# Earlier and wider-spaced stack loads, and a later exponential, in a two-block attention kernel

## The chip, the core and the metric

The kernel runs on one core of a Trainium2 chip. The metric is the device time of one execution in microseconds (us). Engines are named as the profile names them: PE (matmuls; PEld is its weight loads), DVE (VectorE), ACT (ScalarE), POOL (GpSimd) and SP (SyncE, which issues nearly all DMAs here).

## The reference, cut to what matters

Two attention blocks on separate inputs, each 2048 positions of width 640, 32 heads of 20 values. Block A looks at 8 earlier positions, two apart; block B is full attention.

```python
def _A_ref(x, wqkv, wo):                       # H=32, Dh=20, W=8, dil=2
    q, k, v = ...                              # x @ wqkv, split in heads
    idx = pos[:, None] - arange(W)[None, :] * dil
    logits = einsum("bhsd,bhswd->bhsw", q, k[idx]) * scale
    attn = softmax(where(idx >= 0, logits, -1e9))
    return einsum("bhsw,bhswd->bhsd", attn, v[idx]) @ wo

def _B_ref(x, wqkv, wo):
    q, k, v = ...
    p = softmax(einsum("bhqd,bhkd->bhqk", q, k) * Dh ** -0.5)
    return einsum("bhqk,bhkd->bhqd", p, v) @ wo

return concatenate([_A_ref(...), _B_ref(...)], axis=-1)
```

All inputs are float32.

## The kernel before

**Stages.** The projections of both blocks come first (to about 440 us of the profiled execution). They leave q, k and v of both blocks in DRAM scratch tensors (`qa_d`, `ka_d`, `va_d`, `qb_d`, `kb_d`, `vb_d`). Then one loop over 512 steps (`for i in range(NS + LAG)`) does all of block B's attention, and block A's attention is woven into it. Block B's output projection follows (from about 1800 us).

**Block B's loop.** The 32 heads form 8 groups of 4. A group has 4 query chunks of 512 and each chunk 16 key blocks of 128, so a group is 64 steps and a chunk 16. `g` is the group of step `i` and `sub` its step within the group. A step does:

- `b_qk(i)`: four score matmuls (`ps_st<-bq,bk`) and four exponentials on ACT (`e<-ps_st`).
- `b_pv(i - 2)`: the products with the values (`ps_st<-e,vb`). Every second step ACT copies the sum out (`more<-ps_st`) and POOL adds it to the running one (`braw<-braw,more`).
- `b_max(i + 24)`: matmuls of a later chunk (`ps_mx<-bk,bq`), of which DVE takes the row maxima (`mx<-ps_mx`). They are needed before that chunk's exponentials.

The matmuls read **stacks**: `bk` (the keys of a group), `bq` (its queries, by chunk) and `vb` (its values), two buffers of each. Of group g+1 the maxima read `bk` and the first chunk of `bq` from `sub` 40 of group g on. The score matmuls read them from `sub` 0 of group g+1.

**Two side chains of each chunk.** Both go through DRAM and so through SP's queue:

- *Maxima* (`max_rows`): DVE reduces and transposes them (`mtr<-mx`), POOL splits them, SP stores them (`mdr<-mtr`, 4 DMAs) and loads them back as two extra rows of `bq` (`bq<-mdr`, 2 DMAs). That load is due 3 steps before the chunk's first score matmul, which reads it.
- *Normalizing* (`normalize`): SP stores the sums (`s_d<-braw`, due at steps 6, 22, 38 and 54 of a group) and loads them in another layout (`sm<-s_d`, a step later). DVE takes the reciprocal two steps after that (`sm<-sm`). SP stores and broadcasts it (`s_d<-sm`, `rb<-s_d`) and POOL multiplies.

**Order of the work.** Each engine runs its instructions in the order in which the program issues them. `after(n, fn)` puts a call off by n steps; `tick()` at the head of a step runs the calls that are due, in the order in which they were put off. So SP's queue is the order of these calls, and a DMA that has to wait holds up all behind it.

**Block A in the loop.** `a_attention` is a generator of 128 units, 4 for the scores and 4 for the values of each of 16 tiles of 128 positions, nearly all of it POOL work (`akv`, `ao`). `next(a_work)` runs one unit at the steps with `i % 14` in 1, 5, 7, 11. Each unit also moves `a_softmax` of the open tile on by one `yield`: the maximum (DVE `am<-al`), the subtraction (POOL `al<-al,am`), the exponential (ACT `al<-al`), the sums (POOL `am<-al`, `am<-am`), the reciprocal (DVE `am<-am`), the product (POOL). What is left of it when the tile's first unit of values comes (`c == 4`) is run at once there. For tiles 1 to 14 eight units lie between the last scores and that unit, for the first and the last tile only four. Block A's output projection (`a_out`, 15 matmuls `ps_st<-ww,aot` and an ACT copy `ro<-ps_st`) is put into single steps with `i % 6 == 4`.

**The lines that change.** `a_softmax` has one `yield` between the subtraction and the exponential. The loop calls `b_pieces(g + 1)` at `sub == 16` and puts off 21 loads: 4 pieces of `bk` (640, 352, 640, 352 KB), 16 pieces of `bq` (160 and 80 KB in turn) and one of `vb` (760 KB), one each step, so at `sub` 16 to 36.

Of the kernel before, what the change touches and what calls it, by code (L numbers as in the profile page):

```python
# [22 lines left out]
NG = H // GH  # L23
# [35 lines left out]
def attention_pair(ctx, tc, xa, wqk_a, wv_a, wo_a, xb, wqk_b, wv_b, wo_b, oa, ob):  # L59
# [12 lines left out]
    def after(n, fn, *args):  # L72
        due.setdefault(now[0] + n, []).append((fn, args))
# [7 lines left out]
    def tick():  # L81
        now[0] += 1
        for fn, args in due.pop(now[0], ()):
            fn(*args)
# [232 lines left out]
    def pool(out, a, b, op):  # L317
        gp.tensor_tensor(out, a, b, op)
# [12 lines left out]
    def a_softmax(t):  # L331

        _, L, _ = a_t[t]
        if t % (NT // 2) == 0:
            pool(L, L, mask, ALU.add)
        yield
        yield
        m = sb.tile([128, 4, H], F32, tag="am", bufs=2, name="am")
        dve.tensor_reduce(m[:, 0], L.rearrange("p o h -> p h o"), AX.X, ALU.max)
        yield  # L340
        pool(L, L, m[:, 0].unsqueeze(1).to_broadcast([128, WIN, H]), ALU.subtract)
        yield
        act.activation(L, L, AF.Exp, scale=SCALE)
        yield
        pool(m, L[:, :4], L[:, 4:], ALU.add)
        pool(m[:, :2], m[:, :2], m[:, 2:], ALU.add)
        pool(m[:, 0], m[:, 0], m[:, 1], ALU.add)
        yield
        dve.reciprocal(m[:, 0], m[:, 0])
        yield  # L350
        pool(L, L, m[:, 0].unsqueeze(1).to_broadcast([128, WIN, H]), ALU.mult)
# [46 lines left out]
    def a_turn(t, o):  # L398

        b = sb.tile([128, KC, 128], F32, tag="stg", bufs=3, name="turn")  # L400
        d = dr.tile([128, D], F32, tag="tr_d", bufs=2, name="tr_d")

        def back():
            r = sb.tile([128, KC, 128], F32, tag="stg", bufs=3, name="back")
            src = d.rearrange("(b j) (k m c) -> m j k b c", b=4, k=KC, c=32)
            for m in range(4):
                sp.dma_start(r[32 * m:32 * m + 32].rearrange("j k (b c) -> j k b c", c=32), src[m])
            turned.append((now[0] + 3, t, r))
        for k in range(KC):
            after(1 + k, dve.transpose, b[:, k], o[:, k * 128:(k + 1) * 128])  # L410
        after(KC + 2, sp.dma_start, d, b.rearrange("p k c -> p (k c)"))
        after(KC + 5, back)

    def turn_parts():

        if ready_a or not turned or turned[0][0] > now[0]:
            return
        _, t, r = turned.pop(0)
        ot = sb.tile([128, 2, KC, 128], F32R, tag="aot", bufs=1, name="aot")
        gp.tensor_copy(ot[:, 0], r)  # L420
        gp.tensor_tensor(ot[:, 1], r, ot[:, 0].bitcast(F32), ALU.subtract)
        ready_a.append((now[0] + 7, t, ot))
# [62 lines left out]
    def b_pieces(g):  # L485
        k = sb.tile([128, 2, S], F32R, tag="big", bufs=4, name="bk")
        q = sb.tile([128, NQC, 2, 512], F32R, tag="big", bufs=4, name="bq")
        v = sb.tile([128, NKB, VG], F32, tag="vb", bufs=2, name="vb")
        stacks[g] = (q, k, v)
        out = []  # L490
        hs = [slice(g * GH + 2 * r, g * GH + 2 * r + 2) for r in range(2)]

        def add(t, src, runs):
            for r0, s0, n in runs:
                out.append(lambda: sp.dma_start(t[r0:r0 + n].bitcast(F32), src[s0:s0 + n]))
        for r in range(2):
            for r0, s0, n in BK_RUNS:
                add(k[r * HALF:], kb_d[:, hs[r]], [(r0, s0, n)])
        for qc in range(NQC):
            for r in range(2):  # L500
                for r0, s0, n in BQ_RUNS:
                    add(q[r * HALF:, qc], qb_d[qc, :, hs[r]], [(r0, s0, n)])
        return out[:4], out[4:]

    def v_piece(g, b0, b1):

        sp.dma_start(stacks[g][2][:, b0:b1], vb_d[b0 * 128:b1 * 128, g * GH * VC:g * GH * VC + VG]
                     .rearrange("(b p) c -> p b c", p=128))
# [134 lines left out]
    def b_qk(i):  # L643
        u, kb = divmod(i, NKB)
        g, qc = divmod(u, NQC)
        q, k, v = stacks[g]
        P[i] = []
        for pl in range(2):
            w = wide() if pl and i + LEAD >= NS else None
            ps2 = [bank() for _ in range(2)] if w is None else [w[:, 0], w[:, 1]]  # L650
            for r in range(2):
                rows = slice(r * HALF, r * HALF + BM)
                pe.matmul(ps2[r], k[rows, pl, kb * 128:kb * 128 + 128], q[rows, qc, pl], start=True, stop=True)
            if i + LEAD >= NS and i % 2:
                e = sb.tile([128, 2, 512], F32, tag="akv", bufs=4, name="e")
            else:
                e = sb.tile([128, 2, 512], F32, tag="p", bufs=PB, name="e")
            for r in range(2):
                act.activation(e[:, r], ps2[r], AF.Exp, scale=SCALE)
                if w is None:  # L660
                    give(ps2[r])
            P[i].append(e)
            yield

    def b_pv(i):
        u, kb = divmod(i, NKB)
        g, qc = divmod(u, NQC)
        n, part = divmod(kb, 2)
        if part == 0:
            accs[u] = bank()  # L670
        acc = accs[u]
        for j in range(GH):
            pe.matmul(acc[32 * j:32 * j + 32, :], stacks[g][2][:, kb, j * VC:j * VC + 32], P[i][j % 2][:, j // 2],
                      start=(part == 0), stop=(part == 1))
        del P[i]
        if part == 0:
            return
        if n == 0:
            raws[u] = sb.tile([128, 512], F32, tag="raw", bufs=2, name="braw")
            act.copy(raws[u], acc)  # L680
        else:
            more = spare[n % 2][:, n // 2 % 2]
            act.copy(more, acc)
            after(1, pool, raws[u], raws[u], more, ALU.add)
        give(accs.pop(u))
        if kb == NKB - 1:
            last = g == NG - 1
            normalize(raws.pop(u), g, qc * 512, 2 if last else 5, (lambda: out_last(qc)) if last else None)
# [4 lines left out]
    def out_first(qc):  # L693

        o = columns(2)
        outs_b[qc] = o
        for k in range(KC - 1):
            after(1 + 2 * k, split, chunk(o, 0, k), chunk(o, 1, k),
                  ot_b[k * 128:(k + 1) * 128, qc * 512:(qc + 1) * 512], "stg", gp, gp.tensor_copy)
# [71 lines left out]
    def load_out(src, W, halves=range(2)):  # L771
        for h in halves:
            w, more = wide_pieces(src[h], gp)
            W.append(w)
            loads.extend(more)
# [16 lines left out]
    loop[0] = now[0] + 1  # L792
    for i in range(NS + LAG):
        g, sub = divmod(i, NQC * NKB)
        if sub == 16 and g + 1 < NG:
            k_loads, q_loads = b_pieces(g + 1)
            for n, fn in enumerate(k_loads + q_loads + [lambda g=g + 1: v_piece(g, 0, NKB)]):
                after(1 + n, fn)
        if i in (NS - 56, NS - 40):
            out_first((i - NS + 56) // NKB)  # L800
        tick()
        if loads and i % 2:
            loads.pop(0)()
        if i % 14 in (1, 5, 7, 11) and next(a_work, 0) == 0:
            for d in done_a:
                d[0] -= 1
        if done_a and done_a[0][0] <= 0:
            a_turn(*done_a.pop(0)[1:])
        turn_parts()
        if i + LEAD >= NS:  # L810

            for _ in b_qk(i) if i < NS else ():
                pass
            if i % 2:
                b_pv(i - LAG - 1)
                b_pv(i - LAG)
                if fill:
                    fill.pop(0)()
            continue
        qk = b_qk(i) if i < NS else iter(())  # L820
        next(qk, None)
        if i >= LAG:
            b_pv(i - LAG)
        else:
            v_group(*v_late.pop(0))
            if not v_late:
                load_out(wo_a, WO, (1,))

                spare += [sb.tile([128, 2, 512], F32, tag="last0", bufs=2, name="more") for _ in range(2)]
        next(qk, None)  # L830
        mx = b_max(i + LEAD)
        next(mx, None)
        if fill and i % 2 == 0:
            fill.pop(0)()
        elif i % 6 == 4 and not out_piece() and not left_a[0] and not WO_b:
            load_out(wo_b, WO_b)
        next(mx, None)
# [57 lines left out]
```

## Time and profile before

| | us |
|---|---|
| median of 3 runs | 1849.35 |
| the 3 runs | 1849.69, 1845.63, 1849.35 |
| the profiled execution, its own time | 1847.92 |
| its span, first to last instruction | 1846.1 |
| busy: PE / DVE / ACT / POOL | 1797.0 / 1319.3 / 1352.8 / 1214.2 |
| mean granted clock of PE | 0.998 |

The profile's page gives each engine's busy time and share of the span. The view of windows gives the same for stretches of 20 us. The view of waits adds up who waited for whom. The timeline lists instructions in order of time: start, duration, engine, operation, tile written and read, how many alike were merged (x4), and in brackets the idle time of the engine before it and what ended it. "SPq" rows are SP issuing DMAs; their duration is that of issuing, not of moving the data.

### The profile page before, as it was taken

The page shows a single profiled execution, that of the slowest core. Times are in us where ns is not written, and L with a number is a line of the kernel's source. Part 1 is how long each engine was busy: PE and PEld are TensorE (multiplying, and loading weights), DVE is VectorE, ACT ScalarE, POOL GpSimd, SP SyncE. Part 2 cuts the span into 40 slices and gives each one's busy share as a digit, 9 for nine tenths or more (in the row PEclk, how much of TensorE's full clock was granted, in tenths as well). Part 3 has the DMA queues.
Part 4 walks back from the last instruction along what each step waited for, and adds up shares of the span by engine and source line. Part 5 has one row for each costly group of instructions (what it writes and reads, how often), then busy time and mean ns, then how long its engine had stood idle before and what let it go on. Part 6 is the DMA issues. An engine that isn't in the chain of part 4 may idle for free. (4 is left out here: it accounts for less than half of the span.)

```text
span 1846.1 us, 30585 instructions
## 1 busy us (share of the span) xinstructions
PE 1797.0 (97%) x11211; PEld 961.3 (52%) x11211; DVE 1319.3 (71%) x1350; ACT 1352.8 (73%) x2597; POOL 1214.2 (66%) x1072
## 2 busy tenths in 40 slices
PE   9999999999999999999999999999999999999999
PEld 8888888886334343343343333433434434433568
DVE  3100233278898989988989999899888898899500
ACT  4222322224898989988989999899888898899891
POOL 0000075028999999989899899899988873255232
PEclk9999999999999999999999999999999999999999
DMA  6323686655552364336425633553363242021023
GB/s 223 111 93 110 204 301 235 217 170 179 143 154 96 99 180 136 101 114 171 123 83 153 172 96 104 158 153 108 101 189 111 72 119 75 18 69 52 27 70 112
DMA packets 193006, 240.23 MB, mean 130 GB/s; under 512 B 90972, under 2 KB 121308, under 8 KB 191864
## 3 DMA queue, kind: packets, MB, share of 16 engines
q1 hardware_dynamic: 192280, 237.63, 42.7%
q8 instruction: 88, 1.44, 0.3%
q10 hardware_dynamic: 576, 0.66, 0.1%
q14 instruction: 62, 0.51, 0.1%
HBM read 173.29 MB, written 64.91 MB: 129 GB/s over the span
## 5 line engine op out<-in xcount | busy, mean ns | idle before, releaser
L55 DVE TENSOR_REDUCE mx<-ps_mx 128x2 f32<-128x1024 f32 x1024 | 1196.8, 1217 | 139.0 <-PE ps_mx L55 136.7
L55 ACT ACTIVATE e<-ps_st 128x512 f32<-128x512 f32 x2000 | 1061.0, 606 | 57.0 <-PE ps_st L55 27.9
L55 PE MATMUL ps_st<-e,vb 128*32 128x512 f32 x4096 | 544.1, 605 | 0.5
L55 PE MATMUL ps_st<-bq,bk 62*128 62x512 f32 x2000 | 470.8, 455 | 2.6 <-ACT e L55 2.6
L55 PEld LDWEIGHTS ps_st<-bq,bk 62*128 62x128 f32 x2000 | 246.9, 184 | 425.2 <-ACT e L55 411.7
L55 PE MATMUL ps_mx<-bk,bq 60*128 60x512 f32 x2048 | 422.3, 442 | 39.9 <-DVE mx L55 23.4
L55 POOL TENSOR_TENSOR braw<-braw,more 128x512 f32<-128x512 f32 x224 | 287.5, 1284 | 182.7 <-ACT more L55 176.9
L55 POOL TENSOR_TENSOR akv<-akv,aq 128x1280 f32<-128x1280 f32 x64 | 188.1, 2939 | 237.1 <-DMA akv<-ka_d 237.1
L55 PEld LDWEIGHTS ps_mx<-bk,bq 60*128 60x128 f32 x2048 | 193.0, 185 | 208.5 <-DVE mx L55 197.7
L55 POOL TENSOR_TENSOR akv<-akv 128x640 f32<-128x640 f32 (+3 forms) x304 | 281.7, 927 | 23.8
L55 PEld LDWEIGHTS ps_st<-e,vb 128*32 128x32 f32 x4096 | 82.1, 108 | 157.8 <-ACT e L55 81.9
L55 ACT COPY ro<-ps_st 128x320 f32<-128x320 f32 (+1 forms) x92 | 43.5, 473 | 156.8 <-PE ps_st L55 111.6
L55 POOL TENSOR_TENSOR akv<-akv,al 128x1280 f32<-128x1280 f32 x64 | 151.5, 2366 | 0.2
L55 ACT COPY more<-ps_st 128x512 f32<-128x512 f32 x224 | 132.4, 591 | 12.6 <-PE ps_st L55 5.8
L55 PE MATMUL ps_st<-ww,xn 128*128 128x320 f32 x720 | 120.1, 315 | 0.0
L55 PEld LDWEIGHTS ps_st<-ww,xn 128*128 128x128 f32 x720 | 106.6, 188 | 20.9 <-ACT e L55 9.1
L55 POOL TENSOR_TENSOR xn<-stg,xn 128x512 fp32r<-128x512 f32 (+1 forms) x20 | 30.1, 1507 | 96.1 <-ACT xn L55 94.9
L55 DVE TENSOR_TENSOR wc<-stg,wc 128x480 fp32r<-128x480 f32 (+5 forms) x15 | 8.4, 559 | 102.2 <-ACT wc L55 102.1
L55 PE MATMUL ps_st<-ww,aot 128*128 128x320 f32 x480 | 79.7, 318 | 0.0
L55 PEld LDWEIGHTS ps_st<-ww,aot 128*128 128x128 f32 x480 | 71.2, 190 | 12.0 <-ACT e L55 5.5
L55 POOL TENSOR_TENSOR ao<-ao,akv 128x640 f32<-128x640 f32 x48 | 74.7, 1557 | 3.8
L55 DVE TENSOR_TENSOR xl<-stg,xl 128x512 fp32r<-128x512 f32 x12 | 8.3, 688 | 95.9 <-ACT xl L55 95.9
(84 smaller groups left out, 1313.9 us busy)
## 6 DMA issues: line engine op xcount, KB each, us to landing
akv<-ka_d SPq DMA_DIRECT2D x128, 320.0 KB
akv<-va_d SPq DMA_DIRECT2D x128, 320.0 KB
kb_d<-pr SPq DMA_DIRECT2D x20, 512.0 KB
qb_d<-pr SPq DMA_DIRECT2D x20, 512.0 KB
bk<-kb_d SPq DMA_DIRECT2D x16, 640.0 KB
bq<-qb_d SPq DMA_DIRECT2D x64, 160.0 KB
rb<-s_d SPq DMA_DIRECT2D x128, 64.0 KB
stg<-xb SPq DMA_DIRECT2D x12, 512.0 KB
```

Source lines behind the costliest of these rows:

```text
L55: return lambda *a, **k: self.tc.keep_in_program_order(op(*a, **k))
```

## The change

The loads of the next group's stacks are put off from `sub == 4` on, and one is due every second step: the pieces of `bk` at `sub` 4, 6, 8, 10, those of `bq` at 12 to 42, `vb` at 44. In `a_softmax` there is one `yield` more between the subtraction and the exponential, so the exponential and all that follows it come one unit of block A later.

```diff
@@ -339,6 +339,7 @@
         dve.tensor_reduce(m[:, 0], L.rearrange("p o h -> p h o"), AX.X, ALU.max)
         yield
         pool(L, L, m[:, 0].unsqueeze(1).to_broadcast([128, WIN, H]), ALU.subtract)
+        yield
         yield
         act.activation(L, L, AF.Exp, scale=SCALE)
         yield
@@ -792,10 +793,10 @@
     loop[0] = now[0] + 1
     for i in range(NS + LAG):
         g, sub = divmod(i, NQC * NKB)
-        if sub == 16 and g + 1 < NG:
+        if sub == 4 and g + 1 < NG:
             k_loads, q_loads = b_pieces(g + 1)
             for n, fn in enumerate(k_loads + q_loads + [lambda g=g + 1: v_piece(g, 0, NKB)]):
-                after(1 + n, fn)
+                after(1 + 2 * n, fn)
         if i in (NS - 56, NS - 40):
             out_first((i - NS + 56) // NKB)
         tick()
```

## The prediction

> **What bounds the kernel now.** I read the page first, then the waits of the loop (440 to 1740 us), then the windows for stretches that fall behind, then the timeline there. The page puts PE at 97%, but that busy time is modelled, so I looked at what paces an ordinary stretch of the loop:
>
> ```profile
> PE 1797.0 (97%) x11211; PEld 961.3 (52%) x11211; DVE 1319.3 (71%) x1350; ACT 1352.8 (73%) x2597; POOL 1214.2 (66%) x1072
> ...
> 905.32 0.59 ACT L55 COPY more<-ps_st 128x512 f32<-128x512 f32 x1 [0.19 <-PE ps_st L55]
> ...
> 905.80 4.38 ACT L55 ACTIVATE e<-ps_st 128x512 f32<-128x512 f32 x8
> ...
> 910.25 0.59 ACT L55 COPY more<-ps_st 128x512 f32<-128x512 f32 x1
> ```
>
> From one `more` copy to the next, which is two steps, pass 910.25 - 905.32 = 4.93 us, and ACT is busy in them for 0.59 + 4.38 = 4.97 us. So in ordinary steps ACT sets the pace, and time in which ACT stands still there is time lost. That is my unit of price. Neither half of the change shortens ACT's work; it can only remove or add stalls. The waits of the loop have two entries that the change touches:
>
> ```profile
> ACT al L55 <- POOL al L55: 2.4, 1, 2.4
> ...
> DVE sm L55 <- DMA sm<-s_d: 3.1, 2, 1.9
> ```
>
> One wait of block A's exponential for POOL, and two waits of DVE for the sums that come back from DRAM. Each holds an engine that runs in order, and so the whole loop.
>
> **The exponential.** In the first group POOL was late with the subtraction, and ACT stood before the exponential:
>
> ```profile
> 497.66 0.72 POOL L55 TENSOR_TENSOR al<-al,am 128x256 f32<-128x256 f32 x1
> ...
> 498.40 0.42 ACT L55 ACTIVATE al<-al 128x256 f32<-128x256 f32 x1 [2.42 <-POOL al L55]
> ...
> 499.36 0.49 PE L55 MATMUL ps_st<-bq,bk 62*128 62x512 f32 x1 [1.88 <-ACT e L55]
> ...
> 502.95 1.08 ACT L55 ACTIVATE e<-ps_st 128x512 f32<-128x512 f32 x2 [0.71 <-PE ps_st L55]
> ...
> 506.49 0.43 ACT L55 COPY ro<-ps_st 128x320 f32<-128x320 f32 x1 [2.45 <-PE ps_st L55]
> ...
> 587.41 0.43 ACT L55 COPY ro<-ps_st 128x320 f32<-128x320 f32 x1 [1.56 <-PE ps_st L55]
> ...
> 500.00:520.00 20.00, 19.46 (x124) 8.52 (x121) 15.95 (x19) 16.10 (x33) 19.06 (x17) 0.91 0.56 163
> ```
>
> ACT lost 2.42 us, then 0.71, and then at the output projection 2.45 us where the same place later costs 1.56 (row 587.41), so 0.89 more: 2.42 + 0.71 + 0.89 = 4.0 us. The last column but two of the windows row says why there is an aftermath: the granted clock was 0.91 there, PE ran slow after its own wait of 1.88 us. The Trainium skill ("TensorE: Matmul & The Clock Gate", Part 1 and "HAM oscillation") says that PE falls to half clock for a window of about 3.4 us, and only after gaps longer than about 3.4 us. The size agrees, 1 - 0.5 x 3.4 / 20 = 0.915, the threshold does not: 1.88 us was enough. By the page's threshold the aftermath would be chance and this term 2.4 instead of 4.0 us; I go by the rows.
>
> With the added yield the subtraction stays at `i % 14 == 5` and the exponential moves from 7 to 11, so POOL has six steps (some 15 us at 4.93 per two) instead of two. A delay of 2.42 us is covered: **-4.0 us**. The sums, the reciprocal and the product move by a unit too; from sums to reciprocal it stays 4 steps, so DVE has no new wait behind POOL. The exception is tile 15, with four units between: now the exponential, the sums and the reciprocal all fall into one unit, and DVE must wait in its queue, with all later maxima behind it, for ACT and POOL:
>
> ```profile
> 1470.32 0.47 POOL L55 TENSOR_TENSOR am<-al 128x128 f32<-128x128 f32 x1
> ...
> 1470.87 0.65 POOL L55 TENSOR_TENSOR am<-am 128x64 f32<-128x64 f32 x2
> ```
>
> 0.42 + 0.47 + 0.65 = 1.5 us at most, nothing if DVE comes later than ACT by as much. I take the middle, **+0.8 us**. The same at tile 0, before the loop, lies under projection matmuls that do not wait for DVE's next instruction; at nothing, and 1.5 us if that cover fails.
>
> **The loads.** Both DVE waits lie where the 21 pieces are issued now:
>
> ```profile
> 843.25 0.55 SPq L55 DMA_DIRECT2D s_d<-braw  x1
> ...
> 849.56 0.35 SPq L55 DMA_DIRECT2D sm<-s_d  x1
> ...
> 851.20 0.25 DVE L55 RECIPROCAL sm<-sm 128x16 f32<-128x16 f32 x1 [1.17 <-DMA sm<-s_d]
> ...
> 854.85 1.09 ACT L55 ACTIVATE e<-ps_st 128x512 f32<-128x512 f32 x2 [1.42 <-PE ps_st L55]
> ...
> 1347.67 0.54 SPq L55 DMA_DIRECT2D s_d<-braw  x1
> ...
> 1355.74 0.35 SPq L55 DMA_DIRECT2D sm<-s_d  x1
> ...
> 1358.55 0.25 DVE L55 RECIPROCAL sm<-sm 128x16 f32<-128x16 f32 x1 [1.90 <-DMA sm<-s_d]
> ...
> 1362.54 1.08 ACT L55 ACTIVATE e<-ps_st 128x512 f32<-128x512 f32 x2 [2.49 <-PE ps_st L55]
> ...
> 1364.44 0.59 ACT L55 COPY more<-ps_st 128x512 f32<-128x512 f32 x1 [0.82 <-PE ps_st L55]
> ```
>
> From the store of the sums to their load passed 6.3 and 8.1 us, and DVE was held 1.17 and 1.90 us. ACT then lost 1.4 us at the first place and 2.49 + 0.82 = 3.3 us at the second. What makes SP slow there is the pieces:
>
> ```profile
> 651.31 0.36 SPq L55 DMA_DIRECT2D bk<-kb_d  x1
> 651.71 1.46 SPq L55 DMA_DIRECT2D ot_b<-braw  x4
> 653.21 1.99 SPq L55 DMA_DIRECT2D bk<-kb_d  x1
> 655.25 1.00 SPq L55 DMA_DIRECT2D akv<-ka_d  x2
> 661.39 0.67 SPq L55 DMA_DIRECT2D bk<-kb_d  x2
> ...
> SPq L55 <- DMA bk<-kb_d: 5.1, 1, 5.1
> ```
>
> SP issued eight DMAs from 651.31 on (1 + 4 + 1 + 2) and then stood 5.1 us, by the waits, for a `bk` piece. I read it so: the ninth DMA waits until the first has landed, which took 661.39 - 651.31 = 10.1 us. With a piece in every step, SP runs into that again and again and the sums come late. The Trainium skill ("DMA: Bandwidth & Descriptors", Specifications) gives about 27 GiB/s for a DMA engine, and its rule on how many engines a DMA uses gives ten for 40 rows: 640 KB would be some 2.3 us, by estimate. By that figure the pieces could not hold SP and the waits would stay (first rival); the 10.1 us speak against it.
>
> At half the rate a piece of `bk` has 4.93 us to itself, and at `sub` 22 and 38 only `bq` pieces of 160 and 80 KB are left beside the sums. So both waits go: **-1.4 - 3.3 = -4.7 us**. What is late next? Three places, of which I cost two at nothing and one not.
>
> At `sub` 6 to 9 the big pieces now meet the sums of the chunk before; they come singly and the reciprocal waits for program order three steps (7.4 us) behind the store: nothing, 3.3 us a time if not. At `sub` 44 `vb` is queued directly before the stores of the maxima, which lead to `bq<-mdr` and so to the first score matmul at 48. The nearest rows are `vb` before a store of sums, and that load with its reader:
>
> ```profile
> 1555.32 0.39 SPq L55 DMA_DIRECT2D vb<-vb_d  x1
> 1555.80 1.32 SPq L55 DMA_DIRECT2D s_d<-braw  x1
> 1560.89 0.32 SPq L55 DMA_DIRECT2D sm<-s_d  x1
> ...
> 1241.20 0.53 SPq L55 DMA_DIRECT2D bq<-mdr  x2
> ...
> 1246.73 0.40 PE L55 MATMUL ps_st<-bq,bk 62*128 62x512 f32 x2
> ```
>
> Store to load behind `vb` took 5.1 us in all. The load at 1241.20 had 5.5 us to its reader; a load from DRAM took 851.20 - 849.56 = 1.6 us to be usable, which leaves 3.9. Were all 5.1 us added, it would be 1.2 us late here, the tightest of the seven places that I looked at; but part of the 5.1 us the maxima take without `vb` too. Nothing, with 1.2 us as the bad end.
>
> In the first group there is no room. Its load at `sub` 15 comes just in time:
>
> ```profile
> 481.23 0.53 SPq L55 DMA_DIRECT2D bq<-mdr  x2
> ...
> 482.99 0.64 PE L55 MATMUL ps_st<-bq,bk 62*128 62x512 f32 x2 [0.74 <-ACT e L55]
> ```
>
> 1.8 us before its reader. Two pieces now stand in SP's queue shortly ahead of it, at 0.36 us of issuing each (row 651.31) and a little of their data: **+0.8 us**, between nothing and the 3.3 us of the worst stall above.
>
> The sum is -4.0 - 4.7 + 0.8 + 0.8 = **-7.1 us**. Against the profiled execution's own 1847.92 us that is 1840.8. That execution lies 1.4 us under the median of the runs, so against the median it is 1849.35 - 7.1 = **1842.3 us**.
>
> **The rivals.** *The reciprocal's waits only move* to `sub` 9 or 41, or the pieces were never their cause. For it: the three normalizations that the pieces now touch in each group instead of one. Against: half the rate. Then -4.0 + 1.6 = -2.4 us, 1846.9.
>
> *The maxima come late* (the other side). The `bk` pieces at 8 and 10 and `vb` at 44 stand before `mdr` and `bq<-mdr`, and PE, ACT and DVE wait at `sub` 16 and 48. Mechanism: SP held for the eighth DMA before, as at 656.25. It decides from about 3.9 us of added delay, and one hold was 5.1 us. If it costs 1 us at one place in each of six groups, with the 1.6 us of slow clock that followed the first stall (0.71 + 0.89), it is 6 x 2.6 = 15.6 us, so 1849.35 - 7.1 + 15.6 = 1857.9. Against: SP reaches these stores only every 16 steps, and the load then has over 5 us.
>
> *The stalls are chance.* The three runs span 4 us with one program; the fastest, 1845.63, may hold none of the three stalls. Then the median moves by about half, to some 1846.
>
> **How the numbers follow.** About 0.2%, 3.7 us, is what a measurement of this kernel can tell from no change. Chances: the forecast 0.55 (faster), the waits that move 0.20 (same), the late maxima 0.15 (slower), chance stalls 0.10 (half faster, half same). So faster 0.60, same 0.25, slower 0.15. The low end is the fastest run less the sum, 1845.6 - 7.1 = 1838.5. The high end takes in the forecast with its bad ends (-8.7 + 1.5 + 3.3, 1845.5) and the rival of 1846.9, and reaches 1851 into the late maxima, leaving out most of these.
>
> **What would show it.** Right: in the waits of the loop no `ACT al <- POOL al` and no `DVE sm <- DMA sm<-s_d`, SP's waits for `bk<-kb_d` well under their present length, no window below 1.00 in the clock, `bq<-mdr` still several us before its reader. Wrong: an idle PE or ACT at the first score matmul of a chunk (steps 16 and 48), a reciprocal held at `sub` 9 or 41, or DVE held for POOL's sums other than once, at the last tile.

## Result and profile after

The changed kernel takes 1841.84 us (median of 7 runs, 1841.37 to 1843.49) against 1847.59 us before (7 runs, the three above among them, 1844.03 to 1849.69). The ratio is 0.9972 [0.996, 0.9984], so it is faster: the gain of 0.28% is small, but its interval leaves out 1. The profiled execution went from 1847.92 to 1841.84 us and its span from 1846.1 to 1840.0, 6.1 us less.

The engines' busy times on the page of after are nearly those of before:

```profile
PE 1796.4 (98%) x11211; PEld 961.8 (52%) x11211; DVE 1318.5 (72%) x1350; ACT 1356.7 (74%) x2597; POOL 1214.9 (66%) x1072
```

As no engine has less work, the 6.1 us are stalls. The waits of the loop after (total, number of times, longest) no longer hold the two rows of before, `ACT al <- POOL al` and `DVE sm <- DMA sm<-s_d`. Of PE, DVE and ACT two others of 0.4 us or more are new:

```profile
PE ps_st L55 <- DMA bq<-mdr: 2.0, 1, 2.0
...
DVE am L55 <- POOL am L55: 0.4, 1, 0.4
```

SP's own waits for pieces of `bk` in the loop, first before and then after:

```profile
SPq L55 <- DMA bk<-kb_d: 55.9, 19, 5.1
```

```profile
SPq L55 <- DMA bk<-kb_d: 0.5, 1, 0.5
```

SP stood 55.9 us for them in 19 waits, and now 0.5 in one.

**The exponential.** The timeline of after, at the place of the 2.42 us wait:

```profile
498.16 0.72 POOL L55 TENSOR_TENSOR al<-al,am 128x256 f32<-128x256 f32 x1
...
504.65 0.43 ACT L55 COPY ro<-ps_st 128x320 f32<-128x320 f32 x1 [1.55 <-PE ps_st L55]
...
510.04 0.42 ACT L55 ACTIVATE al<-al 128x256 f32<-128x256 f32 x1
```

POOL's subtraction ends at 498.88 and the exponential starts at 510.04 without a wait. The copy `ro` waits the ordinary 1.55 us instead of 2.45.

**The sums.** The timeline of SP and DVE after, at the place of the second wait (group 5):

```profile
1339.78 0.53 SPq L55 DMA_DIRECT2D s_d<-braw  x1
1340.41 2.69 SPq L55 DMA_DIRECT2D back<-tr_d  x4
1343.20 0.58 SPq L55 DMA_DIRECT2D sm<-s_d  x1
...
1353.52 0.24 DVE L55 RECIPROCAL sm<-sm 128x16 f32<-128x16 f32 x1
```

From the end of issuing the store to the load pass 2.9 us, where it was 7.5. The store itself also goes out sooner: 4.3 us ahead of the first score matmul of its step, where it came 0.5 us behind it. The reciprocal does not wait. At this place (`sub` 22) the seven groups that load a next one had 4.3 to 7.9 us before and have 1.2 to 2.9 after. I call this time the store-to-load gap below.

**The new stall.** In the first group, step 16, after:

```profile
477.39 0.67 SPq L55 DMA_DIRECT2D bq<-qb_d  x1
478.16 1.73 SPq L55 DMA_DIRECT2D mdr<-mtr  x4
...
482.11 0.55 SPq L55 DMA_DIRECT2D bq<-mdr  x2
...
483.89 0.70 PE L55 MATMUL ps_st<-bq,bk 62*128 62x512 f32 x2 [2.04 <-DMA bq<-mdr]
```

One piece of `bq`, 0.67 us of issuing, stands directly ahead of the stores of the maxima. The load comes at 482.11 instead of 481.23. Counted from the first score matmul of step 13 that is 1.3 us later (7.64 for 6.35), and PE waits 2.04 us where it waited 0.74 (for ACT), 1.3 us more. After that PE is slow, as the windows show (the last three columns are granted clock, share of the DMA engines and GB/s):

```profile
480.00:500.00 20.00, 17.64 (x110) 6.73 (x104) 15.84 (x16) 15.83 (x31) 19.53 (x15) 0.91 0.50 152
500.00:520.00 20.00, 19.56 (x132) 8.78 (x131) 17.69 (x21) 17.47 (x35) 19.14 (x17) 1.00 0.22 73
```

The low clock that stood in 500 to 520 before is gone, but 480 to 500 now has 0.91. In the first profile of before there was a second stretch at 0.91, 1360 to 1380 us, behind the second wait for the sums; it is at 1.00 in after.

**The balance.** I compared the start of the score matmuls of each step in both traces. At steps 21 and 22 after has 2.03 and 1.99 us less (4.0), at `sub` 26 of group 2 1.27 less, at `sub` 26 and 27 of group 5 2.11 and 1.28 less (together 4.7). At steps 15 and 16 it has 1.31 and 1.42 us more (2.7). -4.0 - 4.7 + 2.7 = -6.0, which is all but 0.1 us of the difference of the spans (smaller differences elsewhere, such as a loop that starts 0.5 us earlier, nearly cancel). The 2.7 us are the 1.3 us of added wait, in step 15, and 1.4 us of slow clock, in step 16.

### The profile page after: what moved, and what is told of

Read it like the earlier page. It is cut to its first block, busy times and chain, and to the rows that moved or that the text cites. A ratio compares the mean times of both kernels' runs of the same rounds, so it can differ in the third digit from the quotient of the medians.

```text
span 1840.0 us, 30597 instructions
## 1 busy us (share of the span) xinstructions
PE 1796.4 (98%) x11211; PEld 961.8 (52%) x11211; DVE 1318.5 (72%) x1350; ACT 1356.7 (74%) x2597; POOL 1214.9 (66%) x1072
```

## The experiments

The profile after cannot tell why the sums came early, nor what each half is worth alone. The prediction's theory was: pieces in every step hold SP, because its ninth DMA waits for the first of eight to land. Against it stand two of its rivals, that the waits only move and that the stalls are chance, and a third explanation: that the place of the pieces matters and not their rate. The text before each measurement was written ahead of the run. Ratios are to the kernel before, with 95% intervals.

**The later exponential alone.**

```diff
         pool(L, L, m[:, 0].unsqueeze(1).to_broadcast([128, WIN, H]), ALU.subtract)
+        yield
         yield
```

> Only the added yield; the loads stay at sub 16, one each step. My theory (each half removes its own stalls): the wait of ACT for POOL at step 21 goes (-4.0 us), the two waits of DVE for the sums at step 26 of groups 2 and 5 stay, one short wait of DVE for POOL's sums at the last tile (+0.4): 1847.6 - 3.6 = 1844.0 us. Rival (the stalls are chance and any new order shakes them): no particular stall goes, 1847.6, with DVE waits at other places than before.

Measured: 1842.9 us (12 runs, 1841.07 to 1847.88), ratio 0.9991 [0.9981, 1.0]. In its waits `ACT al <- POOL al` is gone and the sums' waits remain:

```profile
DVE sm L55 <- DMA sm<-s_d: 5.6, 3, 2.2
```

So the yield removes the exponential's wait. The sums wait three times here and not twice: the new place is group 0 (1.5 us, at 510 us), just behind the stall that went, so part of its price can come back there. By the interval the gain cannot be told from nothing. The runs of this program spread over 6.8 us, and the profiled one is the slowest of them.

**The loads alone, earlier and wider.**

```diff
-        if sub == 16 and g + 1 < NG:
+        if sub == 4 and g + 1 < NG:
...
-                after(1 + n, fn)
+                after(1 + 2 * n, fn)
```

> Only the loads from sub 4 on, every second step; no added yield. My theory: both DVE waits for the sums go (-4.7), the late maxima of the first group cost 2.7 us at steps 15 and 16. During that PE wait POOL works on, so POOL is about 2 us less behind at step 21 and ACT's wait for it shrinks from 2.4 us to under 0.5: in all near 1842, as with both halves. Rival (the halves simply add up): ACT still waits 2.4 us and loses 4.0: 1847.6 - 4.7 + 2.7 = 1845.6.

Measured: 1843.28 us (11 runs, 1841.07 to 1844.97), 0.999 [0.9981, 0.9998]. No wait for the sums is left, and the new wait is there:

```profile
PE ps_st L55 <- DMA bq<-mdr: 2.6, 1, 2.6
```

ACT's wait for POOL is gone here too, without the yield: PE's 2.6 us a few steps earlier held ACT, and POOL had time to catch up. That this is the reason is argued: without the yield, PE's waits of 2.5 us and more there left no wait for POOL, 1.4 us left 1.2, but 1.6 us with the clock at 1.00 (only `bk` moved, below) left all of 2.4. The halves are not independent.

**Wider alone: from `sub` 16, every second step.**

```diff
-                after(1 + n, fn)
+                after(1 + 2 * n, fn)
```

> The loads begin at sub 16 as before but come every second step (to sub 56); no added yield. My theory (what held SP is a piece in every step): both DVE waits for the sums go, SP's waits for bk fall from 55.9 us to under 10, the first group's load of the maxima is as before, ACT's wait at step 21 stays: 1847.6 - 4.7 = 1842.9. Rival (what counts is that the big pieces no longer stand before the sums of step 22): bk still comes at 16 to 22, the waits stay: 1847.6.

Measured: 1842.87 us (12 runs, 1841.46 to 1845.42), 0.9987 [0.9979, 0.9996]. Half the rate is what I had credited, and nearly all of DVE's wait for the sums is gone (0.3 us). But in this run the gap at `sub` 22 is 3.6 to 10.9 us, no shorter than before. SP's queue in group 5:

```profile
1339.53 0.38 SPq L55 DMA_DIRECT2D bk<-kb_d  x1
1340.01 0.53 SPq L55 DMA_DIRECT2D s_d<-braw  x1
1342.40 8.51 SPq L55 DMA_DIRECT2D back<-tr_d  x4
...
1351.45 0.33 SPq L55 DMA_DIRECT2D sm<-s_d  x1
```

A single piece of `bk` stands ahead of the store and the load still comes 10.9 us later. DVE hardly waited, since the store is issued earlier than before (1340.01 for 1347.67). So the rate alone does not make the sums quick; it lets them start sooner. SP still stood 23.2 us for pieces of `bk`, not under 10. And PE waited 1.4 us for `bq<-mdr` in the first group, with no piece ahead of that load: it is late by itself in some executions.

**Earlier alone: from `sub` 4, one each step.**

```diff
-        if sub == 16 and g + 1 < NG:
+        if sub == 4 and g + 1 < NG:
```

> The loads begin at sub 4 but come every step (to sub 24); no added yield. My theory (rate): SP is held for bk as before (over 40 us in all), now ahead of the sums of sub 6 and of the maxima's load at 13; the waits move there, the first group's late maxima cost at least the 2.7 us that they cost at half the rate: 1847 to 1851. Rival (place): the sums of step 22 meet only small pieces, the DVE waits go and nothing new comes but the 2.7 us: 1845.6 or less.

Measured: 1852.57 us (6 runs, 1849.97 to 1856.09), 1.0044 [1.0031, 1.0057], slower. The waits of the loop:

```profile
PE ps_st L55 <- DMA bq<-mdr: 6.6, 1, 6.6
DVE sm L55 <- DMA sm<-s_d: 4.4, 1, 4.4
```

The gap at `sub` 22 is short (1.2 to 4.2 us), but the crowd now stands at `sub` 4 to 24: the first group's maxima are 6.6 us late, and the sums stored at `sub` 6 of group 2 hold DVE at `sub` 10. The waits did move, although SP's waits for `bk` are only 19.9 us in all, not the 40 and more that I expected. At the new place the loads need the lower rate.

**Which DMAs, and is it SP's queue?** The pieces of `bk` of the loop issued by POOL instead, at the steps of before:

```diff
-        def add(t, src, runs):
+        def add(t, src, runs, q=sp):
...
-                out.append(lambda: sp.dma_start(t[r0:r0 + n].bitcast(F32), src[s0:s0 + n]))
+                out.append(lambda: q.dma_start(t[r0:r0 + n].bitcast(F32), src[s0:s0 + n]))
...
-                add(k[r * HALF:], kb_d[:, hs[r]], [(r0, s0, n)])
+                add(k[r * HALF:], kb_d[:, hs[r]], [(r0, s0, n)], gp if g else sp)
```

> The kernel before, with the bk pieces of the loop issued by POOL instead of SP, at the same steps. It tells two reasons for the late sums apart. My theory (SP's queue is held until the DMA eight before has landed): SP's waits for bk are gone, the sums of step 22 are stored and loaded again within some 3 us as elsewhere, no DVE wait at step 26; ACT may wait longer for POOL at step 21, since POOL issues DMAs in between: 1843 to 1846. Rival (the 2 MB themselves fill the DMA engines): the sums take 6 us and more from store to load at sub 22 as before, DVE still waits at step 26.

Measured: 1855.64 us (4 runs, 1852.74 to 1856.52), 1.0047 [1.003, 1.0064]. Part of that is POOL's own time for issuing, which makes its subtraction later (ACT waited 4.7 us for it), so the verdict rests on the gap, not on the time. SP has no wait for `bk` left, and the gap at `sub` 22 is 9.0 to 11.4 us, longer than before:

```profile
1350.56 0.53 POOL L55 DMA_DIRECT2D bk<-kb_d  x1
...
1351.48 0.53 SPq L55 DMA_DIRECT2D s_d<-braw  x1
1352.11 10.58 SPq L55 DMA_DIRECT2D back<-tr_d  x4
...
1363.41 0.35 SPq L55 DMA_DIRECT2D sm<-s_d  x1
...
1366.34 0.25 DVE L55 RECIPROCAL sm<-sm 128x16 f32<-128x16 f32 x1 [2.26 <-DMA sm<-s_d]
```

What SP waits for shows why. These are its waits around the sums of `sub` 22 in group 3, first before (1003 to 1014 us), then here (1008 to 1024 us):

```profile
SPq L55 <- DMA bk<-kb_d: 5.4, 3, 2.7
SPq L55 <- DMA s_d<-braw: 3.0, 1, 3.0
```

```profile
SPq L55 <- DMA s_d<-braw: 9.1, 1, 9.1
```

Before, SP is held for `bk` and then still for the store of the sums to land. With `bk` out of its queue the hold for it is gone, and the store alone takes longer than both. (In group 5, SP stood 3.8 us for pieces of `bq` instead.) My theory falls here as to the gap: it is not the pieces in SP's queue that make it long, but their bytes under way at the time. The small transfers behind them land late from whichever queue the pieces came. The Trainium skill ("DMA: Bandwidth & Descriptors", "Issuing engines are not separate DMA queues") says that transfers issued by any engine end up on the same 16 DMA engines, so that another issuing engine saves only issue time; the gaps of 9.0 to 11.4 us agree.

**Only `bk` moved** to `sub` 4, 6, 8, 10; the rest each step from `sub` 20, as before.

```diff
-        if sub == 16 and g + 1 < NG:
+        if sub == 4 and g + 1 < NG:
...
-            for n, fn in enumerate(k_loads + q_loads + [lambda g=g + 1: v_piece(g, 0, NKB)]):
-                after(1 + n, fn)
+            for n, fn in enumerate(k_loads):
+                after(1 + 2 * n, fn)
+            for n, fn in enumerate(q_loads + [lambda g=g + 1: v_piece(g, 0, NKB)]):
+                after(17 + n, fn)
```

> The kernel before with only the four big pieces moved, to sub 4, 6, 8, 10; bq stays at sub 20 to 35, one each step, vb at 36; no added yield. First theory (a piece in every step holds SP): bq in every step still holds it, the sums of step 22 take 4 us and more from store to load, DVE waits stay possible. Second theory, formed after the runs so far (the bytes of bk on the DMA engines delay the small transfers behind them): store to load at sub 22 falls to 1.2 to 3 us, no DVE wait at step 26; the rest as with the loads alone, the first group's maxima are late: 1842 to 1844.

**Only `bq` moved**, to every second step from `sub` 4 with `vb` after it; `bk` at 16 to 19 as before.

```diff
+            for n, fn in enumerate(k_loads):
+                after(13 + n, fn)
+            for n, fn in enumerate(q_loads + [lambda g=g + 1: v_piece(g, 0, NKB)]):
+                after(1 + 2 * n, fn)
```

> The counterpart: bk stays at sub 16 to 19, one each step, bq comes from sub 4 on, every second step, vb at 36; no added yield. First theory (rate of pieces at SP): between 20 and 35 only every second step has a piece, the sums of step 22 come sooner, under 4 us. Second theory (bytes of bk): store to load at sub 22 stays at 5 us and more and DVE waits at step 26 in some groups; the first group's maxima are a little late from bq: 1846 to 1849.

Measured: with only `bk` moved 1843.46 us (11 runs, 1840.82 to 1845.6), 0.9985 [0.9976, 0.9994]; with only `bq` moved 1844.83 us (11 runs, 1843.02 to 1848.32), 0.9992 [0.9983, 1.0001]. The times alone do not part the two; the traces do. SP's queue at `sub` 22 of group 3, first with `bk` moved, then with `bq` moved, each with its row of waits:

```profile
1000.95 0.55 SPq L55 DMA_DIRECT2D s_d<-braw  x1
1001.54 0.45 SPq L55 DMA_DIRECT2D bq<-qb_d  x1
1002.67 0.35 SPq L55 DMA_DIRECT2D sm<-s_d  x1
...
SPq L55 <- DMA bk<-kb_d: 0.5, 1, 0.5
```

```profile
1007.40 0.55 SPq L55 DMA_DIRECT2D s_d<-braw  x1
1018.42 0.35 SPq L55 DMA_DIRECT2D sm<-s_d  x1
...
DVE sm L55 <- DMA sm<-s_d: 2.4, 3, 1.7
```

With `bk` moved the gaps over the groups are 1.2 to 4.6 us and DVE has no wait for the sums, although the pieces of `bq` still go out in every step from `sub` 20 on. With `bq` moved the gaps stay at 3.1 to 10.5 us and DVE waits three times. So the long gaps come from the four large pieces of `bk` issued just ahead of the sums. Either move also delays the first group's `bq<-mdr` (PE waits 1.6 and 2.5 us for it), and with `bk` moved ACT still waits 2.4 us for POOL.

The gap is one half of the lateness. The other is when the store goes out. The table counts both from the first score matmul of `sub` 22 (a minus is ahead of it, as SP runs ahead of PE), for groups 2 and 5, where DVE waited before:

| run | store issued at | load issued at | DVE's waits for the sums, all |
|---|---|---|---|
| before | 2.7, 0.5 | 9.0, 8.6 | 3.1 |
| wider alone | -1.2, -5.3 | 8.2, 6.1 | 0.3 |
| `bk` issued by POOL | -2.0, -3.1 | 9.3, 8.8 | 4.3 |
| only `bq` moved | 5.9, 0.5 | 9.5, 8.2 | 2.4 |
| only `bk` moved | -0.5, -5.3 | 1.2, -0.2 | 0 |
| the change | -2.2, -4.3 | -0.5, -0.9 | 0 |

The store goes out 3 to 6 us sooner whenever SP is not held for a piece of `bk` in every step from `sub` 16 on. The load comes early only when the pieces are away.

**Taking away the new stall.** Two ways, and both together. First, group 0 keeps the old start:

```diff
-        if sub == 4 and g + 1 < NG:
+        if sub == (4 if g else 16) and g + 1 < NG:
```

> The whole change, but the first group's loads begin at sub 16 (every second step); the other groups' at sub 4. My theory: the added loss at steps 15 and 16 of the first group (2.7 us) came from the pieces ahead of the load of the maxima; it goes, only the short wait there that the kernel before has too (0.8) is left: 1841.8 - 2.7 = 1839.2 us. Rival (the load was late by itself, from block A's weights in SP's queue, and the pieces are not what decides): PE still waits over 1.5 us for bq<-mdr, 1841.8.

Second, the change as it is, with one of the loads of block A's output weights (`stg<-wo_a`), the last one, due at step 11, put off to step 13:

```diff
-        if loads and i % 2:
+        if loads and i % 2 and i != 11:
```

> The whole change, and the last piece of block A's output weights is loaded two steps later (not at step 11 but at 13), so that it stands behind the stores of the maxima in SP's queue. My theory: before those stores SP waits for the buffer of that piece, which POOL frees; without it the load of the maxima comes 1 to 2 us earlier although the stack pieces stay, and PE's wait of 2.0 us for it goes: 1839 us. Rival (the stack pieces alone make the load late): PE still waits over 1.5 us, 1841.8.

Both edits:

> The whole change with both amendments: the first group's loads from sub 16 on, and the last piece of block A's output weights two steps later. My theory: no wait for bq<-mdr, for the sums or for the subtraction is left in the loop, 1838.5 to 1839.5 us, and the runs lie within 2 us of each other. Rival (other waits take their place): not under 1841.

Measured: 1838.07 us (5 runs, 1837.06 to 1838.61), 0.9957 [0.9944, 0.9969]; 1838.46 us (5 runs, 1837.37 to 1842.16), 0.9963 [0.9948, 0.9977]; 1838.42 us (5 runs, 1837.11 to 1839.56), 0.9958 [0.9945, 0.9971]. With the old start for group 0 the wait shrank to 0.4 us:

```profile
PE ps_st L55 <- DMA bq<-mdr: 0.4, 1, 0.4
```

With the weights' load put behind it, the queue reaches the maxima earlier:

```profile
475.79 1.73 SPq L55 DMA_DIRECT2D mdr<-mtr  x4
479.83 0.54 SPq L55 DMA_DIRECT2D bq<-mdr  x2
480.41 0.36 SPq L55 DMA_DIRECT2D stg<-wo_a  x1
```

479.83 instead of 482.11, and no wait. Either edit is enough, and both together bring no more. In none of the three profiles does PE's clock fall in the loop. The three were measured with another set of runs of before (median 1845.16, against 1847.59 for the change), and the intervals of their ratios overlap with that of the change, so that they are faster rests on the traces: the span of the first is 1836.2 us, 3.8 less than that of the change.

The place was tight already. Where no piece stands ahead of it, PE's wait for this load is 0 to 1.4 us over the profiles; with pieces ahead, and the weights where they were, it is 1.6 to 6.6.

**Chance?** The kernel before, unchanged, profiled once more.

> The kernel before, unchanged, for a second profiled execution, since its times spread over 7 us. If the stalls are fixed by the order of the work, the same three show: ACT for POOL at step 21, DVE for the sums at step 26 of groups 2 and 5. If they are near misses that each execution decides anew, some are missing or stand in other groups, but at the same steps (21 and 26), and the span differs by their sum.

Measured: 1845.29 us, one run. The stalls recur in the same places:

```profile
DVE sm L55 <- DMA sm<-s_d: 3.0, 2, 1.8
...
ACT al L55 <- POOL al L55: 2.2, 1, 2.2
```

but not with the same aftermath. Its timeline and windows around the exponential and the first of the sums:

```profile
497.39 0.42 ACT L55 ACTIVATE al<-al 128x256 f32<-128x256 f32 x1 [2.21 <-POOL al L55]
...
503.98 0.43 ACT L55 COPY ro<-ps_st 128x320 f32<-128x320 f32 x1 [1.55 <-PE ps_st L55]
...
490.00:510.00 20.00, 17.97 (x123) 7.98 (x120) 14.97 (x14) 15.55 (x32) 19.37 (x14) 1.00 0.62 160
...
840.00:860.00 20.00, 17.63 (x112) 6.22 (x108) 16.77 (x19) 15.95 (x31) 18.79 (x16) 0.91 0.62 177
```

ACT stood 2.21 us and then lost nothing more: `ro` has its ordinary 1.55, the clock stayed at 1.00. In the first profile of before the same stall had cost 4.0 us. This time the clock fell after the wait near 849 us, where it had not fallen in the first profile. In these two profiles the places of the stalls are the same and their costs are not.

## Why the prediction was right, and where it was not

The predicted time was 1842.3 us and the measured median is 1841.84. That they lie 0.5 us apart is in part luck: four more runs of before brought its median from 1849.35 to 1847.59, and the medians differ by 5.75 us, the spans by 6.1, where the sum said 7.1. For the profiled execution the sum gave 1840.8, and it took 1841.84. The steps:

- **The exponential, -4.0:** right, -4.0 by the score matmuls, and the separate run of the yield shows that it removes this wait. But the price holds for that execution. Where the clock does not fall, as in the second profile of before, the stall costs 2.2 us; in the run of the loads alone it vanished by itself.
- **The sums, -4.7:** the size was right (1.27 and 3.39 us at the two places; only the second had a low clock in before), **the mechanism was right by half**. I wrote that pieces in every step hold SP, and that half the rate frees it. That is so for when the store goes out: half the rate in the old place brought it 3.9 and 5.8 us forward, and DVE's waits fell from 3.1 to 0.3 us. It is wrong for the time from store to load, which I put to the same hold: half the rate left the gap at 3.6 to 10.9 us, and with SP free of `bk` it was 9.0 to 11.4, of which the store's own landing took 9.1 in group 3. Only moving `bk` away brought it to 1.2 to 4.6. The prediction set an estimate of 2.3 us for a piece against the 10.1 us seen and took the 10.1 as evidence for the hold. They show that SP was held, and also that bytes were slow to land, which is the part that I did not follow to the sums.
- **What widening is for:** in the old place it lets the store go out in time; at the new place the loads need it. The loads moved without it are slower than before, 1.0044 [1.0031, 1.0057].
- **The first group's load, +0.8 between 0 and 3.3:** the **mis-sized term**. It cost 2.7. I had counted two issues of 0.36 us and a little of their data; the load came 1.3 us later by the loop's own steps, and PE stood 1.3 us longer. The other 1.4 us are the low clock (0.91 in 480 to 500), an aftermath that I had counted for the stall that goes and not for the one that comes. The pieces are not all of it: with no piece ahead the wait was up to 1.4 us in one profile.
- **Tile 15, +0.8 between 0 and 1.5:** DVE waited 0.4 us for POOL, and no score matmul around it started later.
- **`sub` 6 to 9, nothing:** no wait there in after. But it is no large reserve: one store and load at `sub` 6 of group 2 took 9.1 us, and the run without widening was held just there.
- **`vb` ahead of the maxima, nothing:** no wait, but near. The tightest place, group 4, in the timeline of after:

```profile
1233.66 0.37 SPq L55 DMA_DIRECT2D vb<-vb_d  x1
...
1234.46 4.63 SPq L55 DMA_DIRECT2D mdr<-mtr  x4
1241.57 0.54 SPq L55 DMA_DIRECT2D bq<-mdr  x2
...
1243.60 0.42 PE L55 MATMUL ps_st<-bq,bk 62*128 62x512 f32 x2
```

The four stores of the maxima took 4.63 us to issue behind `vb`, and the load is now 2.0 us before its reader, where it had 5.5. With 1.6 us for a load to be usable, 0.4 us are left.

Of the signs that I named, "no window below 1.00" and "`bq<-mdr` several us before its reader" were missed, both by the new stall and the second also at group 4. Of the rivals, *the waits only move* is not what the change does, but it is what the earlier start alone does. *The maxima come late* was the right mechanism at one place instead of six. *The stalls are chance* falls as to their places and holds in part for their price. It may be why the yield alone, at 0.9991 or 1.7 us of 1845.88, shows less than the 4.0 us that its stall cost in one trace, and so may the new wait for the sums in its group 0; the interval is too wide to say.

What stays open is why an 8 KB store needs up to some 10 us to land behind these pieces (SP's longest wait for one is 6.6 us before and 10.2 with `bk` issued by POOL), that is, which part of the path it queues in. No run separates that.

## What to carry to other kernels

Before crediting a change of rate, ask which transfer's bytes are under way when a small one with a deadline goes out, and move the large one to where nothing small is due; the queue that stands may be only half of the cause. When loads are moved earlier, look at the first pass of the loop by itself, as its deadlines have the least room: keeping the old place for that pass alone took PE's wait there from 2.04 to 0.4 us and the low clock behind it away. Give a stall that is added the same aftermath in the sum as one that is removed.

## What the runs showed of the hardware

PE's clock fell after short waits, and not always, and the length of the wait does not decide. After the 1.88 us of before's first profile the next 20 us had 0.91, after the 2.04 us of the changed kernel 0.91, and after the 1.4 us of the run with the wider loads alone 0.91 again. After the 1.68 us of before's second profile,

```profile
498.35 0.50 PE L55 MATMUL ps_st<-bq,bk 62*128 62x512 f32 x1 [1.68 <-ACT e L55]
```

and after the 1.6 us of the run with only `bk` moved, they had 1.00.

What decides can be read from the thirteen profiles together. In each, the time between two changes of the clock is a whole multiple of 3.413 us to within 0.01 us, so the changes lie on a fixed grid. Here are the two stretches of the grid around the fall in before's first profile, and then the stretch at the same place in the second, where the clock did not fall. The first figure behind the comma is PE's busy time, the last but two the clock:

```profile
498.04:501.45 3.41, 2.09 (x15) 0.97 (x15) 1.32 (x2) 3.05 (x7) 3.33 (x3) 1.00 0.49 148
501.45:504.87 3.42, 3.42 (x15) 2.10 (x11) 2.27 (x2) 1.87 (x4) 3.34 (x3) 0.50 0.78 204
```

```profile
497.19:500.60 3.41, 2.25 (x15) 0.97 (x15) 1.48 (x2) 3.21 (x8) 3.33 (x3) 1.00 0.51 158
```

Cut in this way, the loops (440 to 1740 us) of the thirteen profiles have 4917 stretches at full clock. In 15 of them PE was busy for 2.10 us or less, and the clock was halved right after every one; in the other 4902 it was busy for 2.12 us or more, and the clock was halved after none. So a wait costs the clock when enough of it falls into one stretch, and where the grid lies differs from one execution to the next, which accounts for the same stall at 4.0 us in one profile and 2.2 in another. This is read off the profiles, whose PE times are modelled; no run was made to test it.

The Trainium skill ("TensorE: Matmul & The Clock Gate", "What's actually happening") calls the window that is watched free-running, and the grid agrees. Its bound, an idle window of about 3.4 us, does not agree: 1.3 us without work in a window of 3.4 was enough.
